# S4 and a dense mixture of experts on one core: the waits of S4's kernel chain, rewritten

## The chip, the core and the metric

The kernel runs on one core of a Trainium2 chip. Its engines work side by side, each through its own instructions in order: TensorE (matrix products; PE in the profile, its weight loads PEld), VectorE (DVE), ScalarE (ACT), GpSimd (POOL) and SyncE (SP), which here issues most of the DMAs. Products land in PSUM banks and are read out by ScalarE or VectorE. The metric is the device time of the whole kernel in microseconds; less is better.

## The reference

The input is one sequence of 2048 tokens of 512 channels. It is normalized, and the output is the sum of the input, an S4 branch and a mixture of experts:

```python
x = A_u
xn = _layernorm(x, axis=-1)
return x + _A_ref(xn, ...) + _B_ref(xn, B_w_gate, B_w1, B_w2)

# _A_ref: S4, a convolution over time for each channel, and a skip
P = exp(dt * A * arange(L));  K = einsum("dn,dnl,dn->dl", Cc, P, dB).real
y = irfft(rfft(up) * rfft(Kp))[:L] + u * Dskip
# _B_ref: K = E = 8, so each token goes through each of the 8 experts
gates = softmax(xf @ w_gate)
out = sum over e of gates[:, e] * (silu(xf @ w1[e]) @ w2[e])     # F = 1792
```

The change touches only the S4 branch: how the convolution kernel K (with the skip added at its first tap) is scaled and handed on.

## The kernel before

**Two works in one program.** The mixture of experts is nearly all of TensorE's work: 8 experts by 4 blocks of 512 tokens, each block in four parts of hidden columns (DQS: 2, 2, 2 and 1 pairs), each part in four slots. A slot issues one or two sets of first products (`product`, hb), a few second products (`pop`, y), and the activations between. 512 slots cover the whole, and `clock["slot"]` counts them; `now()` returns the count. All operands are split into a high and a low f16 part, so a product is three matmuls, and each tensor needs a high part (ScalarE) and a low part (VectorE).

**S4 beside it.** S4 goes in 32 chunks of 16 channels (NCH = 32). Its instructions are put into the queues while the mixture's slots are written out: at the end of each slot from the 46th on, `bg_run` first polls the small generators in `polled` once each, in order (`s4_pe` first), and then draws VectorE work from the generator `bg` until a quota is used up: SHARE = 0.905 of the TensorE time that the planner counts for the slot, less the VectorE time that it counts for the mixture. So the whole order is fixed when the program is written out, and no engine can overtake it. What is left of S4 before the last token block of the last expert is put out by `bg_until("s4")` with no mixture work between (line 1335 ff.; called in the main loop at the end).

**One chunk c.** VectorE makes tables (`s4_tables`, from a basis made for every two chunks). TensorE forms the kernel product kgen from them (`s4_kernel`, L803) in the small bank, the one PSUM buffer with the tag s4, which all of S4's products share (ps_s, bufs=1). ScalarE copies it to ksb (`s4_kernel_out`, L810), VectorE adds the skip (`s4_skip`, L816), and `s4_kernel_turn` squares ksb for its sum per partition (L822) and turns the tile over DRAM (kd, then four loads kt: L826, L828). `pow2_total` sums the rows over the partitions with a product with ones (L180) and gives, after its read (L175), the scale (`s4_kscale`, L186 to L191). Then come the high and low part of the turned kernel (`s4_khigh` L841, `s4_klow` L846), its transform (`s4_kf`, L884), the convolution on VectorE (`s4_conv`, L899 to L937), the split of its result z (`s4_zhigh`, `s4_zlow`), the back product (`s4_back`, L958) and the output (`s4_out`). The input's transform is `s4_uf` (L870).

**Waits in slots.** S4's order is made by generators that yield until a key was set enough slots ago. `until(key, more=m)` goes on once now() > slot of the key + m; without m that is two slots later. `hold(stamp)` goes on once the slot is past stamp. A bare `yield None` is one slot. `bank_wait` waits until the small bank's last product was read out: `bank_free` puts the pending read into ScalarE's queue and says yes one slot later. Since one bank serves all, `s4_pe` puts its products in a fixed cycle: kf(c), back(c-1), kernel(c+2), uf(c+1). The wait in front of kernel(c+2), line 1045, is

```python
yield from until(("kl", c + 1), more=-1)
```

with "kl" set by s4_klow, the low part of the chunk before. `s4_ksplit(c)` runs the steps from the copy to the low part, line 1064 ff., and is one of the polled generators; `s4_dve(c)` waits for "kn" (the kernel product of the chunk before, since the tables have one buffer), makes tables(c+2), waits for "kf" and runs the convolution of c.

Of the kernel before, what the change touches and what calls it, by code (L numbers as in the profile page):

```python
# [9 lines left out]
F32 = mybir.dt.float32  # L10
F16 = mybir.dt.float16
BF16 = mybir.dt.bfloat16
I32 = mybir.dt.int32
AF = mybir.ActivationFunctionType
ALU = mybir.AluOpType
AX = mybir.AxisListType
PSUM = bass.MemoryType.PSUM

P = 128
# [14 lines left out]
def s4_moe_kernel(  # L34
# [15 lines left out]
    nc = tc.nc  # L50
    V, S, T = nc.vector, nc.scalar, nc.tensor
# [10 lines left out]
    NCH = us.shape[0]  # L62
    DC = 16
    NI = NT
# [3 lines left out]
    cp = ctx.enter_context(tc.tile_pool(name="cp", bufs=1))  # L68
    sb = ctx.enter_context(tc.tile_pool(name="sb", bufs=2))
# [31 lines left out]
    clock = {"slot": 0, "pe": 0.0, "pe0": 0.0, "dve": 0.0, "dve0": 0.0, "left": 0.0,  # L101
             "act": 0.0, "act0": 0.0, "pe1": 0.0, "actleft": 0.0, "two": False}
# [33 lines left out]
    wgt = cp.tile([P, KT, E], F32, name="wgt")  # L136
    dskq = cp.tile([P, NCH, 4], F32, name="dskq")
    V.memset(dskq, 0.0)
    sgnt = cp.tile([P, 2], F32, name="sgnt")
    mult_t = cp.tile([P, 2, NK], F32, name="mult_t")  # L140
    dt_all = cp.tile([P, D], F32, name="dt_all")
# [498 lines left out]
    s4 = {}  # L640
# [11 lines left out]

    def s4_twiddle():

        f = s4["angle"] = sb.tile([P, P + 1], F32, tag="b0", name="angle", bufs=1)
        V.tensor_copy(f, s4["odd"])

        def sines():
            tw = s4["tw"] = sb.tile([P, 2, P + 1], F32, tag="b1", name="twid", bufs=1)
            S.activation(tw[:, 1], f, AF.Sin, scale=math.pi / (4 * P))  # L660
            S.activation(tw[:, 0], f, AF.Sin, scale=-math.pi / (4 * P), bias=halfpi)
        act_later.append((clock["slot"] + 1, sines))
# [132 lines left out]
    def s4_kernel(c):  # L795
        tb = s4["tb", c]
        take_bank(lambda: s4_kernel_out(c))
        kg_ = ps_s.tile([P, 4, 64], F32, tag="s4", name=f"kgen{c}")
        for dg in range(4):
            for cc in range(2):  # L800
                for dsb in range(4):
                    d = dsb * 4 + dg
                    T.matmul(kg_[32 * dsb:32 * dsb + 32, dg, :], tb[:, cc, 0, d, :],  # L803
                             tb[:, cc, 1:3, d, :], start=(cc == 0), stop=(cc == 1))
        s4["kgen"] = kg_
        clock["pe"] += 1.2

    def s4_kernel_out(c):
        ksb = s4["ksb"] = sb.tile([P, 8, 4, NS], F32, tag="ksb", name=f"ksb{c}", bufs=1)
        S.copy(ksb, s4["kgen"].rearrange("p g (j m) -> p j g m", j=8))  # L810
        clock["act"] += at_(256)
        s4["kc", c] = now()

    def s4_skip(c):

        V.tensor_tensor(s4["ksb"][:, 0, :, 0], s4["ksb"][:, 0, :, 0], dskq[:, c, :], op=ALU.add)  # L816

    def s4_kernel_turn(c):
        ksb = s4["ksb"]
        row = s4["krow", c] = sb.tile([P, 1], F32, tag="krow", name=f"krow{c}", bufs=2)  # L820
        junk = sb.tile([P, 2, DC * NI], F16, tag="kh", name=f"ksq{c}", bufs=1)
        S.activation(junk[:, 0].bitcast(BF16), ksb.rearrange("p j g m -> p (j g m)"), AF.Square, accum_out=row)  # L822
        clock["act"] += at_(256)
        kt = sb.tile([P, 4, 4 * NI], F32, tag="kt", name=f"kt{c}", bufs=1)
        kd = kds[c % 2]
        nc.sync.dma_start(kd, ksb.rearrange("p (j r) g m -> p j (r g m)", r=2))  # L826
        for jh in range(4):
            nc.sync.dma_start(kt[32 * jh:32 * jh + 32],  # L828
                              kd[:, jh, :].rearrange("(s x) c -> x s c", s=4))
        s4["kt", c] = kt.rearrange("p s x -> p (s x)")  # L830

    def s4_kscale(c):


        ks = s4["ks", c] = sb.tile([P, 2], F32, tag="ksc", name=f"ksc{c}", bufs=4)
        pow2_scale(ks[:, 0:1], s4["kst", c], f"k{c}")
        pow2_inverse(ks[:, 1:2], ks[:, 0:1], ZSH - DSH)
# [39 lines left out]
    def s4_kf(c):  # L877
        take_bank()
        kf = ps_s.tile([P, 2, 2, DC * NS], F32, tag="s4", name=f"kf{c}")
        kh = s4["kh", c].rearrange("p y (s r x) -> p y r s x", s=4, r=2)  # L880
        for a in range(2):
            for r in range(2):
                for n, (x, y) in enumerate(((0, 0), (1, 0), (0, 1))):
                    T.matmul(kf[:, a, r], dfth[:, x, 4 * r + 1 - a, :], kh[:, y, r],  # L884
                             start=(n == 0), stop=(n == 2))
        clock["pe"] += 0.68
        k4 = sb.tile([P, 4, 2, DC, NS], F32, tag="k4", name=f"k4{c}", bufs=1)
        S.copy(k4[:, 2:4].rearrange("p a r d i -> p (a r d i)"), kf.rearrange("p a r d -> p (a r d)"))
        bank["at"] = now()
        s4["k4", c] = k4  # L890
# [59 lines left out]
    def s4_back(c):  # L950
        zh = s4["zh", c]
        take_bank(lambda: s4_out(c))
        yp = ps_s.tile([P, 2, DC, NS], F32, tag="s4", name=f"yp{c}")
        for r in range(2):
            n = 0
            for a in range(2):
                for x, y in ((0, 0), (1, 0), (0, 1)):
                    T.matmul(yp[:, r].rearrange("p d i -> p (d i)"), dfth[:, x, 4 * r + 2 + a, :], zh[:, y, a, r],  # L958
                             start=(n == 0), stop=(n == 5))
                    n += 1  # L960
        s4["yp", c] = yp
        clock["pe"] += 0.68
# [8 lines left out]
    def at_(n):  # L971

        return n / 1050 + 0.17
# [5 lines left out]
    def hold(stamp):  # L979

        while clock["slot"] <= stamp:
            yield None

    def now():
        return clock["slot"]
# [28 lines left out]
    def bank_wait():  # L1014
        while not bank_free():
            yield None

    def until(*keys, more=1):

        for key in keys:  # L1020
            while key not in s4 or now() <= s4[key] + more:
                yield None

    def s4_pe():


        for c in range(-2, NCH + 1):
            if 0 <= c < NCH:
                if c:
                    yield from until(("z at", c - 1))  # L1030
                yield from until(("kl", c))
                yield from bank_wait()
                s4_kf(c)
                s4["kf", c] = now()
                yield None
            if c > 0:
                yield from until(("zl", c - 1))
                yield from bank_wait()
                s4_back(c - 1)
                s4["back", c - 1] = now()  # L1040
                yield None
            if c + 2 < NCH:
                yield from until(("tab", c + 2))
                if c > -2:
                    yield from until(("kl", c + 1), more=-1)
                yield from bank_wait()
                s4_kernel(c + 2)
                s4["kn", c + 2] = now()
                polled.append(s4_ksplit(c + 2))
                yield None  # L1050
                yield from bank_wait()
                yield from until(("kc", c + 2))
            if 0 <= c + 1 < NCH:
                if c >= 0:
                    yield from until(("v3", c))
                yield from until(("ul", c + 1))
                yield from bank_wait()
                s4_uf(c + 1)
                s4["uf", c + 1] = now()
                yield None  # L1060
        yield from bank_wait()
        done.add("s4")

    def s4_ksplit(c):

        yield from until(("kc", c), more=0)
        s4_skip(c)
        yield 0.2
        yield from hold(now() + 1)
        if c:  # L1070
            yield from until(("kf", c - 1), more=0)
        s4_kernel_turn(c)
        yield None
        yield from hold(now())
        yield from bank_wait()
        s4["kst", c] = pow2_total(s4["krow", c], 1, f"k{c}", lambda: s4.update({("read", c): now()}))
        s4["total", c] = now()
        yield None
        while ("read", c) not in s4:
            bank_free()  # L1080
            if ("read", c) not in s4:
                yield None
        yield from until(("read", c), more=0)
        s4_kscale(c)
        yield 0.6
        yield None
        if c:
            yield from until(("kf", c - 1), more=0)
        s4_khigh(c)
        yield None  # L1090
        yield None
        s4_klow(c)
        s4["kl", c] = now()
        yield tt_(256)
# [77 lines left out]
    for pr in range(3, NPR):  # L1172
        for h in range(2):
            n = 2 * (pr - 3) + h
            tag, bufs = ("sE", 1) if n == 0 else ("sCB", 3) if n < 4 else ("stg", 4)
# [593 lines left out]
```

## Time and profile before

| | |
|---|---|
| time, median of 3 runs | 2445.02 us (2444.57 to 2445.96) |
| profiled execution | 2446.37 us; span 2444.6 us, first to last instruction |
| PE busy | 2331.7 us, 95% of the span |
| VectorE busy | 1751.4 us, 72% |
| ScalarE busy | 1464.6 us, 60% |
| GpSimd busy | 339.2 us, 14% |
| granted TensorE clock, mean | 0.974 of full speed |

A row of a timeline is: start in us, duration in us, engine, line, operation, output<-inputs, shape, count; in brackets the idle time before it and what ended it. A row by stretch has, for each engine, its busy time and its instructions in brackets. A row of the groups has a count, the busy time, the mean in ns of one, and then the idle time of the engine before them. The time strip cuts the span into 40 slices of 61 us and gives each engine's busy tenths. A row of waits is: who waited, for whom, us in total, times, longest.

### The profile page before, as it was taken

How to read it: one execution, taken by the hardware profiler on the slowest of the kernel's cores; microseconds unless marked ns; L12 is line 12 of the kernel's file. 1: busy time of each engine (PE TensorE's matmuls, PEld its weight loads, DVE VectorE, ACT ScalarE, POOL GpSimd, SP SyncE). 2: the span in 40 equal slices, each digit the busy share in tenths (PEclk: the TensorE clock that was granted, in tenths of full speed). 3: DMA queues.
4: the chain of work that ended last, by engine and by line, in shares of the span. 5: the costliest groups of instructions: out<-in, count | busy, mean ns of one | idle time of the engine just before them, and what ended most of it. 6: DMA issues, size and time to landing. Idle time of an engine off the chain costs nothing. (4 is left out here: it accounts for less than half of the span.)

```text
span 2444.6 us, 46072 instructions
## 1 busy us (share of the span) xinstructions
PE 2331.7 (95%) x18289; PEld 1559.0 (64%) x18289; DVE 1751.4 (72%) x3492; ACT 1464.6 (60%) x2587; POOL 339.2 (14%) x396
## 2 busy tenths in 40 slices
PE   8999999999999999999999999999999999995259
PEld 4666666666666666666666666666666666664135
DVE  8855875768946797767966697658876588757951
ACT  7676765657666576556666566665665576543123
POOL 0001011120122111011111111111111111110012
PEclk9999999999999999999999999999999999997579
DMA  7686555655667466545666455654655554442127
GB/s 263 193 252 173 143 138 123 149 96 144 147 139 155 80 149 152 127 100 116 142 139 141 84 142 138 137 118 93 147 131 131 120 132 94 76 87 53 22 33 177
DMA packets 325433, 316.33 MB, mean 129 GB/s; under 512 B 183584, under 2 KB 219936, under 8 KB 324768
## 3 DMA queue, kind: packets, MB, share of 16 engines
q1 hardware_dynamic: 268768, 219.24, 30.7%
q0 software_dynamic: 55872, 93.61, 24.3%
q8 instruction: 143, 2.34, 0.4%
q14 instruction: 74, 0.61, 0.1%
q10 hardware_dynamic: 576, 0.52, 0.1%
HBM read 201.88 MB, written 66.06 MB: 110 GB/s over the span
## 5 line engine op out<-in xcount | busy, mean ns | idle before, releaser
L1406 PE MATMUL hb<-xop,w1s 128*128 128x256 f16 x9114 | 1074.1, 273 | 0.4 <-ACT scC L1625 0.3
L1406 PEld LDWEIGHTS <-w1s 128*128 128x128 f16 x9114 | 882.9, 98 | 176.6 <-issue 1.9
L1389 PE MATMUL y<-w2s,ahl 128*128 128x512 f16 x1792 | 679.6, 379 | 0.0
L1390 PE MATMUL y<-w2s,ahl 128*128 128x512 f16 x1792 | 679.4, 379 | 0.0
L1391 PE MATMUL y<-w2s,ahl 128*128 128x512 f16 x1792 | 679.4, 379 | 0.0
L1391 PEld LDWEIGHTS <-ahl 128*128 128x128 f16 x1792 | 175.4, 98 | 211.7 <-issue 0.6
L1596 POOL DMA_DIRECT2D scC<-sE x124 | 116.4, 939 | 1286.3 <-ACT sE L1625 1122.7
L1435 DVE SCALAR_TENSOR_TENSOR ahl<-fa,sc,ahl 128x512 f16<-128x512 f32 (+1 forms) x262 | 179.0, 684 | 154.8 <-ACT ahl L1426 154.2
L1390 PEld LDWEIGHTS <-ahl 128*128 128x128 f16 x1792 | 175.4, 98 | 161.5 <-issue 0.3
L1389 PEld LDWEIGHTS <-ahl 128*128 128x128 f16 x1792 | 175.4, 98 | 161.4 <-issue 0.3
L1422 ACT ACTIVATE fa<-hb,sc 128x512 f32<-128x512 f32 (+1 forms) x252 | 160.5, 637 | 194.7 <-PE hb L1406 194.2
L1435 DVE SCALAR_TENSOR_TENSOR ahl<-scB,sc,ahl 128x512 f16<-128x512 f32 x124 | 84.6, 682 | 196.4 <-ACT ahl L1426 173.7
L1640 ACT COPY hb<-hb 128x512 f32<-128x512 f32 x124 | 64.1, 517 | 234.9 <-PE hb L1406 234.7
L1435 DVE SCALAR_TENSOR_TENSOR ahl<-scC,sc,ahl 128x512 f16<-128x512 f32 x124 | 84.5, 681 | 160.4 <-ACT ahl L1426 146.4
L1426 ACT ACTIVATE ahl<-fa,sc 128x512 f16<-128x512 f32 (+1 forms) x262 | 175.7, 671 | 8.5
L1630 ACT COPY hb<-hb 128x512 f32<-128x512 f32 x124 | 64.3, 519 | 179.5 <-PE hb L1406 179.2
L1596 POOL DMA_DIRECT2D scB<-sE x124 | 107.2, 865 | 415.1 <-ACT scB L1625 307.2
L785 DVE TENSOR_TENSOR ta<-tb,zr 128x64 f32<-128x64 f32 (+2 forms) x192 | 131.8, 687 | 6.0
L791 DVE TENSOR_TENSOR tb<-ta,tt 128x64 f32<-128x64 f32 (+2 forms) x192 | 132.0, 688 | 5.6
L925 DVE TENSOR_TENSOR s<-s,tm 128x672 f32<-128x672 f32 (+6 forms) x224 | 127.7, 570 | 7.8
L788 DVE TENSOR_TENSOR tt<-tb,zi 128x64 f32<-128x64 f32 (+2 forms) x192 | 130.5, 680 | 0.0
L1367 POOL DMA_DIRECT2D oacc<-ye x108 | 95.8, 1331 | 247.4 <-ACT ye L1364 245.7
(267 smaller groups left out, 2547.0 us busy)
## 6 DMA issues: line engine op xcount, KB each, us to landing
xop<-xd SPq DMA_DIRECT2D x210, 256.0 KB, 3.6
pp<-in_w_dram SPq DMA_DIRECT2D x98, 512.0 KB, 4.3
raw<-in_w_dram SPq DMA_DIRECT2D x56, 512.0 KB, 5.1
oacc<-ye POOLq DMA_DIRECT2D x108, 256.0 KB, 6.2
scC<-sE POOLq DMA_DIRECT2D x93, 256.0 KB, 4.3
scB<-sE POOLq DMA_DIRECT2D x93, 256.0 KB, 4.0
raw<-in_w_dram SPq DMA_DIRECT2D x52, 256.0 KB, 4.1
raw<-in_w_dram SPq DMA_DIRECT2D x104, 128.0 KB, 4.0
```

The lines of the kernel that those rows point to most:

```text
L785: V.tensor_tensor(ta, tin, zrv, op=ALU.mult)
L788: V.tensor_tensor(tt, tin[:, ::-1], ziv, op=ALU.mult)
L791: V.tensor_tensor(tout, ta, tt, op=ALU.add)
L925: V.tensor_tensor(s3[:, :, m:], s3[:, :, m:], tm, op=ALU.add)
L1389: T.matmul(y, lhs[0], w2s[pr][:, 0, fh, :], start=(c == 0), stop=False)
L1390: T.matmul(y, lhs[0], w2s[pr][:, 1, fh, :], start=False, stop=False)
L1391: T.matmul(y, lhs[1], w2s[pr][:, 0, fh, :], start=False, stop=(c == NF - 1))
L1406: T.matmul(dst[:, q, :], w1s[pr][:, a, wo, k * P:(k + 1) * P], xop[:, xo, b, k, :], start=(first_mm and q == 0 and n == 0), stop=(n == 5), ...
L1422: S.activation(fa, src[:, :n], AF.Silu, scale=w1_unscale(e, d if whole else prs[0]))
L1426: S.activation(ahl[:, 0, :n], fa, AF.Copy, scale=scales[e][:, 3:4])
L1435: V.scalar_tensor_tensor(ahl[:, 1, :n], fa, sc[:, 3:4], ahl[:, 0, :n], op0=ALU.mult, op1=ALU.subtract)
L1596: nc.gpsimd.dma_start(dst, src, accum_op=ALU.add)
```

## The change

The square that gives the kernel's sum per partition is taken from the small bank, at the copy, ahead of the skip; its elementwise output goes to ksb and is overwritten by the copy. The sum of the skip's squares, made once for all chunks (dsk2), is added to the row when the skip is added. So the sum is that of the squares of kernel and skip, and no longer that of the squares of their sum; it only sets a power of two for scaling. In ksplit a hold is shortened, a bare yield and a second hold go, and the turn waits for the low part of the chunk before (kl) and no longer for its transform (kf). In s4_pe the next kernel product waits for the turn ("ke", a new key) and the read of the total ("read") of the chunk before, and no longer for its low part ("kl").

```diff
+    dsk2 = cp.tile([P, NCH], F32, name="dsk2")
...
     def s4_twiddle():
+        q = sb.tile([P, NCH, 4], F32, tag="b2", name="dskx", bufs=1)
+        V.tensor_tensor(q, dskq, dskq, op=ALU.mult)
+        V.tensor_reduce(dsk2, q, axis=AX.X, op=ALU.add)
...
     def s4_kernel_out(c):
         ksb = s4["ksb"] = sb.tile([P, 8, 4, NS], F32, tag="ksb", name=f"ksb{c}", bufs=1)
+        row = s4["krow", c] = sb.tile([P, 1], F32, tag="krow", name=f"krow{c}", bufs=2)
+        S.activation(ksb.rearrange("p j g m -> p (j g m)"), s4["kgen"].rearrange("p g x -> p (g x)"), AF.Square, accum_out=row)
         S.copy(ksb, s4["kgen"].rearrange("p g (j m) -> p j g m", j=8))
-        clock["act"] += at_(256)
+        clock["act"] += 2 * at_(256)
         s4["kc", c] = now()
...
     def s4_skip(c):
+        row = s4["krow", c]
         V.tensor_tensor(s4["ksb"][:, 0, :, 0], s4["ksb"][:, 0, :, 0], dskq[:, c, :], op=ALU.add)
+        V.tensor_tensor(row, row, dsk2[:, c:c + 1], op=ALU.add)
...
     def s4_kernel_turn(c):
         ksb = s4["ksb"]
-        row = s4["krow", c] = sb.tile([P, 1], F32, tag="krow", name=f"krow{c}", bufs=2)
-        junk = sb.tile([P, 2, DC * NI], F16, tag="kh", name=f"ksq{c}", bufs=1)
-        S.activation(junk[:, 0].bitcast(BF16), ksb.rearrange("p j g m -> p (j g m)"), AF.Square, accum_out=row)
-        clock["act"] += at_(256)
         kt = sb.tile([P, 4, 4 * NI], F32, tag="kt", name=f"kt{c}", bufs=1)
...
         s4["kt", c] = kt.rearrange("p s x -> p (s x)")
+        s4["ke", c] = now()
...
                 if c > -2:
-                    yield from until(("kl", c + 1), more=-1)
+                    yield from until(("ke", c + 1), ("read", c + 1), more=0)
                 yield from bank_wait()
                 s4_kernel(c + 2)
...
         yield from until(("kc", c), more=0)
         s4_skip(c)
-        yield 0.2
-        yield from hold(now() + 1)
+        yield 0.3
+        yield from hold(now())
         if c:
-            yield from until(("kf", c - 1), more=0)
+            yield from until(("kl", c - 1), more=0)
         s4_kernel_turn(c)
-        yield None
-        yield from hold(now())
         yield from bank_wait()
         s4["kst", c] = pow2_total(s4["krow", c], 1, f"k{c}", lambda: s4.update({("read", c): now()}))
```

More of the change, by code (lines that the diff above doesn't have):

```diff
@@ L827, in s4_kernel_turn @@
         for jh in range(4):
-            nc.sync.dma_start(kt[32 * jh:32 * jh + 32],
-                              kd[:, jh, :].rearrange("(s x) c -> x s c", s=4))
+            nc.sync.dma_start(kt[32 * jh:32 * jh + 32], kd[:, jh, :].rearrange("(s x) c -> x s c", s=4))
         s4["kt", c] = kt.rearrange("p s x -> p (s x)")
+        s4["ke", c] = now()
     def s4_kscale(c):
```

## The prediction

> **What bounds the kernel now.** I read the time strip of the page first, then the busy time by stretch, then TensorE's order at the seam, then who waits for whom.
>
> ```profile
> PE   8999999999999999999999999999999999995259
> DVE  8855875768946797767966697658876588757951
> ```
>
> TensorE is full up to slice 36 and then has three poor slices of 61 us each. The same stretches in numbers (columns: length, then busy us of PE, weight loads, VectorE, ScalarE, GpSimd, then granted clock, DMA share, GB/s):
>
> ```profile
> 400.00:2200.00 1800.00, 1799.57 (x14240) 1210.30 (x14239) 1318.31 (x2563) 1121.96 (x2004) 277.55 (x318) 1.00 0.56 125
> 2229.90:2354.30 124.40, 25.24 (x353) 21.99 (x352) 111.09 (x235) 17.52 (x41) 0.21 (x1) 0.51 0.11 19
> 2248.00:2284.00 36.00, 6.41 (x101) 5.62 (x101) 33.80 (x70) 3.68 (x11) 0.00 (x0) 0.50 0.10 15
> 2284.00:2314.00 30.00, 6.41 (x101) 5.62 (x101) 28.14 (x57) 4.31 (x11) 0.00 (x0) 0.50 0.12 18
> ```
>
> From 400 to 2200 us TensorE never rests and VectorE has a quarter of its time free. From 2229.9 to 2354.3 it is the reverse: this is bg_until("s4"), which empties the rest of S4 before the last token block, with no MoE work to lie beside it. VectorE sets the pace there (33.80 of 36 us, then 28.14 of 30). TensorE's rows at the two edges, and the kernel products between:
>
> ```profile
> 313.11 1.10 PE L803 MATMUL kgen<-tb 128*32 128x64 f32 x64
> ...
> 2211.72 1.10 PE L803 MATMUL kgen<-tb 128*32 128x64 f32 x64
> ...
> 2229.07 0.83 PE L958 MATMUL yp<-zh,dfth 128*128 128x128 f16 x12
> ...
> 2314.45 1.93 PE L803 MATMUL kgen<-tb 128*32 128x64 f32 x64 [14.19 <-ACT st_k L175]
> ...
> 2352.94 1.59 PE L958 MATMUL yp<-zh,dfth 128*128 128x128 f16 x12 [12.19 <-ACT ysb L966]
> 2354.32 2.77 PE L1406 MATMUL hb<-xop,w1s 128*128 128x256 f16 x12
> ```
>
> So of 32 chunks 29 had their kernel product before the seam (the first at 313, the 29th at 2211.72), three came after it, and the seam costs 2354.3 - 2229.7 = 124.6 us. How fast S4 runs beside the MoE decides how much is left there: 28 periods took (2211.72 - 313.11) / 28 = 67.8 us each.
>
> What sets that period? One chunk in mid-kernel, in order of time: its kernel product, uf, the square, the total, the low part of its transform, and then the next kernel product and the first step of VectorE's next tables:
>
> ```profile
> 1186.90 1.10 PE L803 MATMUL kgen<-tb 128*32 128x64 f32 x64
> ...
> 1202.27 0.83 PE L870 MATMUL uf<-uh,dfth 128*128 128x128 f16 x12
> 1202.94 0.27 PE L1406 MATMUL hb<-xop,w1s 128*128 128x256 f16 x1
> ...
> 1213.20 0.40 ACT L822 ACTIVATE ksq<-ksb 128x256 bf16<-128x256 f32 x1
> ...
> 1221.86 0.17 PE L180 MATMUL tot_k<-krow,ones 128*128 128x1 bf16 x1
> 1221.89 0.81 PE L1406 MATMUL hb<-xop,w1s 128*128 128x256 f16 x6
> ...
> 1245.06 0.48 DVE L846 SCALAR_TENSOR_TENSOR kh<-kt,ksc,kh 128x256 f16<-128x256 f32 x1
> ...
> 1253.22 1.10 PE L803 MATMUL kgen<-tb 128*32 128x64 f32 x64
> ...
> 1255.45 0.07 DVE L765 MEMSET tb<- 128x16 f32 x1
> ```
>
> One period is 1253.22 - 1186.90 = 66.3 us. VectorE begins the next tables at 1255.45, behind the product at 1253.22 (the tables have one buffer, which that product reads), and the product by the old rule waits for the low part at 1245.06. VectorE is out of S4 work meanwhile: it was busy 39.08 of 41 us before this hole and 3.99 of 19 us in it, with TensorE full in both:
>
> ```profile
> 1195.00:1236.00 41.00, 41.00 (x294) 26.89 (x292) 39.08 (x72) 27.04 (x49) 3.44 (x4) 1.00 0.59 146
> 1236.00:1255.00 19.00, 19.00 (x193) 13.34 (x192) 3.99 (x7) 12.59 (x23) 1.81 (x3) 1.00 0.45 111
> ```
>
> So S4 is held by a chain of one-slot waits, not by work.
>
> **The old chain in slots.** The waits are written in slots, so I count them in the code. (A step whose key must be one slot old comes at +1, by until's default at +2.) With the kernel product in slot K: its copy K+1, skip K+2, then hold(now() + 1) and the turn with the square K+5; uf K+3, kf K+4, back product K+5; a bare yield and a hold, K+7, where ksplit itself releases the bank that the back product left; total K+8, read K+9, scale K+10, high part K+12, low part K+14. s4_pe is polled ahead of ksplit, so it sees the low part at K+15: the next kernel product. Fifteen slots in 66.3 us make 4.42 us a slot; the mean of 67.8 us has a slot added here and there, where another total wants the bank.
>
> **The change, part by part.**
> 1. Square from the small bank at K+1, ahead of the copy, and gone from the turn. ScalarE does as many instructions as before. L822 took 0.40 us from SBUF; read from PSUM I bound it by nothing saved and 0.4 us more, and take the same. It holds the bank less than 1 us longer inside a slot of 4.42 us. What it removes: ScalarE's square no longer stands behind VectorE's skip.
> 2. The row add and dsk2: one small VectorE instruction per chunk. Its nearest rows are below (L816, 159 ns), so 32 x 0.16 = 5 us of VectorE over the whole kernel, plus two once; bounds 2 and 10 us. Hidden under TensorE in the MoE stretch.
> 3. hold(now()), no bare yield and no second hold: the turn is at K+4 at the earliest and the total can follow in the same slot. At K+4 kf has just taken the bank, at K+5 the back product; released by ksplit at K+5, so the total is at K+6, its read K+7: two slots won.
> 4. The turn now waits for the low part of the chunk before (it reuses kt). The recurrence low part to low part is turn +1, read +2, scale +3, high +5, low +7: 7 slots, so it allows 31 us.
> 5. The next kernel product stands behind turn and read: K+8 instead of K+15. That is the large edit.
> The turn moves its five DMAs on SP with it. They are as many as before; kd still has its skip two slots ahead, and kt must be there four slots (17.7 us) after the turn instead of seven. SP waits on the kd write 112.4 us over 32 turns, 3.5 us each, and kt lands 1.8 us after issue, so the cover holds; were it gone, ScalarE would stand at the high part. The rows for 2 and for this, from the groups by line, SyncE's waits, the view of tile kt and TensorE's waits:
>
> ```profile
> L816 DVE TENSOR_TENSOR ksb<-ksb,dskq 128x4 f32<-128x4 f32 x32 | 5.1, 159 | 2.0 <-ACT ksb L810 1.9
> SPq L828 <- DMA kd<-ksb: 112.4, 32, 8.5
> DMA to landing us min/median/max: 1.6/1.8/4.1
> PE hb L1406 <- ACT scC L1625: 0.3, 1, 0.3
> ```
>
> **What is late next.** With the product allowed at K+8 the tables of the chunk after are ready too late for that: VectorE's work becomes the limit. Uncontended it needed 33.80 us for a chunk with a basis and 28.14 us without, 31 us on average. In the MoE stretch 1800 / 67.8 = 26.5 chunks took 26.5 x 31 = 822 us of 1318, so the MoE takes 496 / 1800 = 0.276 of VectorE. At the 39.08 / 41 = 0.953 that it reached in the dense part, a chunk needs 31 / (0.953 - 0.276) = 45.8 us, or 10.4 slots. TensorE's order must fit into that. Counted from the slot Z in which a convolution ends: z's high part Z+1, its low part Z+3, back product Z+5 (two behind its key), bank released and kernel product Z+7, its copy Z+8, uf Z+10, total Z+11, and the next kf behind the next convolution's end by two, so Z+12 or Z+13. It fits, with up to a slot lost where total and kf meet at the bank: **10.5 to 12 slots, 47 to 53 us.**
>
> Does S4 then end before the seam? From the first kernel product to the seam are 2229.7 - 313.1 = 1917 us. After the last kernel product two convolutions without tables remain; by the waits above 3 + 8 + 8 + 7 = 26 slots, 115 us. At 50 us the need is 31 x 50 + 115 = 1665 us, 250 us in hand. The break-even period is (1917 - 115) / 31 = 58 us, 13.1 slots. So all of S4 hides, and the rest of the speed is worth nothing.
>
> **The sum**, on the profiled execution (2446.4 us, span 2444.6; the median of the runs, 2445.0, is 1.4 lower):
> - the seam goes: -124.6;
> - its TensorE work comes to lie between MoE products: 3 kernel products at 1.10, 4 uf, 4 kf and 5 back products (as large as a uf) at 1202.94 - 1202.27 = 0.67, 4 totals at 1221.89 - 1221.86 = 0.03: 3.3 + 8.7 + 0.1 = +12.1;
> - after the seam TensorE started at half clock (0.51 granted): 12 products took 2.77 us. By the rows at 1202.94 (1 in 0.27) and 1221.89 (6 in 0.81) a further one is 0.108 us, so 12 take 1.46: -1.3.
>
> 2446.4 - 124.6 + 12.1 - 1.3 = 2332.6; less 1.4 for the median: **2331 us**.
>
> **The rivals.**
> - **S4 gets faster, but not enough** (7 in 100): a wait that I missed keeps 14 slots, 62 us. Before, 31 x 67.8 + 115 - 1917 = 300 us too much became a seam of 124.6. At 62 us there are 120 too much, so 50 us of seam, worth 45 net: 2376. For it: stretches in which the bank is shared with the weights' totals. Against: it needs over 13.1 slots, and I count at most 12.
> - **VectorE runs late and TensorE feels it** (small form, 5 in 100): dense for some 1500 us instead of two thirds of each period. In the dense 41 us above TensorE had no gap, and the only wait of the MoE products on ScalarE is the 0.3 us shown. A stall of 1% there, which I set as its size, is 15 us: 2346.
> - **The same, beyond the gain** (slower, 4 in 100): at the low parts of the activations (L1435), which the y products need. It decides where stalls pass the 114 us won, in 1500 us, 7.6%. That needs a VectorE demand of 1.08 of its time; at a period of 46 us mine is (31 + 0.276 x 46) / 46 = 0.95. At 10% it would be 2331 + 150 = 2481.
> - **GpSimd's adds starve** (2 in 100). They are the accumulating DMAs scC and scB, each issue 0.86 us and at most 1.92 us, by the view of tile scC:
>
> ```profile
> L1596 POOL DMA_DIRECT2D scC<-sE x124: 859/859/1917, 97.2 to 2422.0; - x124
> DMA to landing us min/median/max: 2.7/4.2/11.8
> ```
>
> If a dense VectorE doubled each landing, ScalarE would take scC later, and a stall of, say, 0.2 us in each of some 170 adds (two per block of 17.6 us) is 34 us: 2365. The Trainium skill, "SBUF — State Buffer", section "SBUF: two separate sides", speaks for this rival: VectorE in a 2-port mode locks GpSimd out, so that it can't write descriptors. By that rule the added load would show in the issue times. The trace agrees little: the median equals the minimum.
> - **It doesn't do what it says** (3 in 100): the planner's VectorE quota, not the chain, holds the period; 2445. Against: the 19 us with VectorE at 3.99.
>
> **How the numbers follow.** All of S4 hidden, without stalls: 79 in 100, and 2320 to 2340 as its own range (the floor is the sum without the 12.1). The small stalls bring it to 84, and the range reaches to 2352 for them; the others stay out. About 0.2%, 5 us, is what a measurement of this kernel can tell from no change. Faster: 79 + 7 + 5 + 2 = 93; same 3; slower 4.
>
> **What would show it.** Right: strip of PE at 9 through slice 38; kernel products 47 to 53 us apart; no idle stretch before the last block; VectorE at 9 until about 1950 us and then at 3 or 4. Right in 3 and 5: total six to eight slots ahead of where it was, product next to VectorE's convolution end. Wrong: products still 62 us or more apart (a wait missed), or TensorE's waits on ahl, hb copies or scC over 10 us in total (VectorE or ScalarE late).

## The result, and the profile after

| | before | changed |
|---|---|---|
| median | 2444.80 us of 4 runs | 2334.26 us of 4 runs (2332.68 to 2335.29) |
| ratio to before, 95% interval | | 0.9547 (0.953 to 0.9563) |
| span of the profiled execution | 2444.6 us | 2332.7 us |

The change saves 110.5 us; 2331 was forecast. First the page of the changed kernel, the lines of PE and VectorE: busy time and share, then the strip of 40 slices (58 us each now).

```profile
PE 2317.6 (99%) x18289; PEld 1547.9 (66%) x18289; DVE 1747.6 (75%) x3526; ACT 1467.5 (63%) x2587; POOL 340.4 (15%) x396
...
PE   8999999999999999999999999999999999999999
...
DVE  8864889889998999888999889999899741441111
```

TensorE's three poor slices are gone. VectorE does the same work (1747.6 us against 1751.4) but stands at 8 or 9 from slice 5 to slice 31 and is nearly idle at the end. In stretches (length; then PE, weight loads, VectorE, ScalarE, GpSimd busy; clock, DMA share, GB/s):

```profile
400.00:1750.00 1350.00, 1348.37 (x11270) 912.46 (x11268) 1216.17 (x2469) 870.23 (x1578) 207.77 (x237) 1.00 0.59 129
1950.00:2230.00 280.00, 280.00 (x1895) 185.08 (x1894) 79.41 (x113) 150.86 (x251) 42.75 (x49) 1.00 0.40 88
2244.50:2332.70 88.20, 84.07 (x535) 52.17 (x533) 14.79 (x26) 34.08 (x60) 24.92 (x29) 0.99 0.67 147
```

While S4 lasts VectorE is busy 1216 of 1350 us, 90%, where it was 73%; afterwards 28%. The last token block is the third row: it begins at 2244.5, straight behind the block before, instead of at 2354.3, and its first 12 products take 1.47 us instead of 2.77. The first and the last kernel product of S4, its last back product and the first products of the last block, from TensorE's timeline:

```profile
313.24 1.10 PE L807 MATMUL kgen<-tb 128*32 128x64 f32 x64
...
1823.27 1.10 PE L807 MATMUL kgen<-tb 128*32 128x64 f32 x64
...
1925.38 0.83 PE L962 MATMUL yp<-zh,dfth 128*128 128x128 f16 x12
...
2244.51 1.47 PE L1408 MATMUL hb<-xop,w1s 128*128 128x256 f16 x12
```

The mean period is (1823.27 - 313.24) / 31 = 48.7 us, and S4 is over at 1926 us, 318 us ahead of the last block. One period from the middle, all engines, in order of time:

```profile
816.38 1.10 PE L807 MATMUL kgen<-tb 128*32 128x64 f32 x64
...
820.72 0.39 ACT L815 ACTIVATE ksb<-kgen 128x256 f32<-128x256 f32 x1
...
824.03 0.42 DVE L941 TENSOR_TENSOR z<-zq 128x256 f32<-128x256 f32 x1
...
825.96 0.15 DVE L824 TENSOR_TENSOR krow<-krow,dsk 128x1 f32<-128x1 f32 x1
...
826.73 0.07 DVE L769 MEMSET tb<- 128x16 f32 x1
...
831.34 0.48 DVE L850 SCALAR_TENSOR_TENSOR kh<-kt,ksc,kh 128x256 f16<-128x256 f32 x1
...
840.24 0.17 PE L181 MATMUL tot_k<-krow,ones 128*128 128x1 bf16 x1
...
867.03 1.10 PE L807 MATMUL kgen<-tb 128*32 128x64 f32 x64
```

Read it against the old period: VectorE ends a convolution at 824.45 and begins the next tables at 826.73, since the product that frees the tables' buffer came at 816.38. The low part of the chunk before (831.34) now falls behind that product. The square (L815) stands ahead of the copy. TensorE's waits over the whole kernel:

```profile
PE tp L357 <- ACT xhl L347: 7.2, 1, 7.2
PE hb L1408 <- ACT scC L1627: 1.6, 6, 0.5
PE hb L1218 <- POOL ident masks.py:199: 1.4, 1, 1.4
```

Only the second of these is new in size: 1.6 us in six places where it was 0.3 in one.

### The profile page after: what moved, and what is told of

It reads as the page before. It is cut to its first block, busy times and chain, and to the rows that moved or that the text cites. A ratio compares the mean times of both kernels' runs of the same rounds, so it can differ in the third digit from the quotient of the medians.

```text
span 2332.7 us, 46118 instructions
## 1 busy us (share of the span) xinstructions
PE 2317.6 (99%) x18289; PEld 1547.9 (66%) x18289; DVE 1747.6 (75%) x3526; ACT 1467.5 (63%) x2587; POOL 340.4 (15%) x396
## 4 chain that ended last, share of the span: by engine, by line
PE 97%; ACT 2%; DVE 0%; issue 0%; DMA 0%; SPq 0%; DVEq 0%; ACTq 0%
PE hb L1408 42%; PE y L1393 16%; PE y L1392 16%; PE y L1391 16%; PE hb L1680 2%; PE kgen L807 1%; PE uf L874 1%; PE kf L888 1%; PE yp L962 1%; ACT ye L1366 1%; PE tp L282 0%; ACT ahl L1428 0%; DMA ut0c<-in_u_dram 0%; ACT scB L1424 0%; ACT fa L1424 0%
## 5 line engine op out<-in xcount | busy, mean ns | idle before, releaser
L1437 DVE SCALAR_TENSOR_TENSOR ahl<-fa,sc,ahl 128x512 f16<-128x512 f32 (+1 forms) x262 | 178.9, 683 | 138.4 <-ACT ahl L1428 137.8
L1437 DVE SCALAR_TENSOR_TENSOR ahl<-scB,sc,ahl 128x512 f16<-128x512 f32 x124 | 84.5, 682 | 165.9 <-ACT ahl L1428 164.4
L1437 DVE SCALAR_TENSOR_TENSOR ahl<-scC,sc,ahl 128x512 f16<-128x512 f32 x124 | 84.4, 681 | 127.3 <-ACT ahl L1428 122.9
```

The source lines that it names most:

```text
L1437: V.scalar_tensor_tensor(ahl[:, 1, :n], fa, sc[:, 3:4], ahl[:, 0, :n], op0=ALU.mult, op1=ALU.subtract)
```

## The experiments

The theory to be tried, called the pace theory below: the time depends on one number, the mean period p of the kernel products beside the mixture. What 31 p + 115 us exceeds 1917 us by is left over at the last block, 0.41 us of seam for each us, nine tenths of it lost; below 58 us nothing is won any more. Its first rival: each edit pays its share of the slots that it saves.

### The square alone

The kernel before, with the change's edits of s4_twiddle, s4_kernel_out and s4_skip (dsk2 among them), and in s4_kernel_turn only this:

```diff
-        row = s4["krow", c] = sb.tile([P, 1], F32, tag="krow", name=f"krow{c}", bufs=2)
-        junk = sb.tile([P, 2, DC * NI], F16, tag="kh", name=f"ksq{c}", bufs=1)
-        S.activation(junk[:, 0].bitcast(BF16), ksb.rearrange("p j g m -> p (j g m)"), AF.Square, accum_out=row)
-        clock["act"] += at_(256)
```

> The kernel before with only the square moved: taken from the small bank at the copy, the skip's squares added to the row; all waits as before. Pace theory: no wait in slots is shortened, so the period stays 67.8 us and the time 2445 us (2441 to 2449). Rival, the square behind the skip held the chain: some us less per period, 2430 us or less.

Measured: 2446.31 us, ratio 1.0006 (0.9997 to 1.0016). Moving the square is worth nothing by itself. By the code the new turn needs it all the same: the old square's junk tile takes kh's one buffer, which the transform of the chunk before still reads, so a turn ahead of that transform must not write it.

### The one wait alone

The kernel before, with two edits:

```diff
         s4["kt", c] = kt.rearrange("p s x -> p (s x)")
+        s4["ke", c] = now()
...
-                    yield from until(("kl", c + 1), more=-1)
+                    yield from until(("ke", c + 1), ("read", c + 1), more=0)
```

> The kernel before with only the one wait changed: the next kernel product stands behind the turn and the read of the total of the chunk before. Square at the turn, both holds, and the turn behind the transform of the chunk before stay as they were. Pace theory: the total comes later (turn behind kf, then three slots), yet the read is done before VectorE's tables call for the product, so the period is 48 to 53 us and the time 2334 us (2330 to 2340). Rival, the shorter chain in ksplit is needed as well: a period of over 58 us and a seam, 2350 us or more.

Measured: 2332.65 us, ratio 0.9544 (0.9528 to 0.956), the whole gain. The period is (2021.43 - 312.82) / 31 = 55.1 us by these rows of TensorE's timeline, two to seven us longer than I expected but under 58, and S4 ends at 2144.5 us:

```profile
312.82 1.10 PE L803 MATMUL kgen<-tb 128*32 128x64 f32 x64
...
2021.43 1.10 PE L803 MATMUL kgen<-tb 128*32 128x64 f32 x64
...
2143.70 0.83 PE L959 MATMUL yp<-zh,dfth 128*128 128x128 f16 x12
```

So the shorter chain in ksplit is not needed for the gain. VectorE is busy 83% from 400 to 1650 us here (1040 of 1250), less than its quota of 0.905 allows, so a wait still holds this period; which one is open.

### All but that wait: 13, 14 and 15 slots

The changed kernel, with the old key put back; more is -1 here, 0 in the second run, 1 and 2 in the last two:

```diff
-                    yield from until(("ke", c + 1), ("read", c + 1), more=0)
+                    yield from until(("kl", c + 1), more=-1)
```

> The changed kernel with one line put back: the next kernel product waits for the low part of the chunk before again; square, holds and turn stay as changed. Pace theory (the time depends only on the period p of the kernel products: what 31 p + 115 us exceeds 1917 us by becomes a seam of 0.41 us per us, worth nine tenths of that): product 13 slots after the last one instead of 15, 57.5 us and 1.5 us for slots lost at the bank, 59 us; 27 us too much, a seam of 11 us, 2344 us (2332 to 2352). Rival, each edit pays its share of the slots: 2 slots of 7 give two sevenths of the 110 us won, 2413 us.

Measured: 2343.87 us, ratio 0.9587 (0.9572 to 0.9601): without the wait, the other edits bring 101 of the 110 us. The period is (2164.82 - 312.46) / 31 = 59.8 us. Just over the break-even, a rest of S4 is left; the first and the last kernel product, the last back product and the first product of the last block:

```profile
312.46 1.10 PE L807 MATMUL kgen<-tb 128*32 128x64 f32 x64
...
2164.82 1.10 PE L807 MATMUL kgen<-tb 128*32 128x64 f32 x64
...
2250.21 1.59 PE L962 MATMUL yp<-zh,dfth 128*128 128x128 f16 x12 [6.57 <-ACT ysb L970]
2251.60 2.76 PE L1408 MATMUL hb<-xop,w1s 128*128 128x256 f16 x12
```

> As the run with the product behind the low part, and one slot later still: 14 slots. Pace theory: 62 us and 1.5 us lost at the bank, 63.4 us; 31 x 63.4 + 115 - 1917 = 163 us too much, a seam of 68 us, worth 61: 2395 us (2375 to 2410). Rival, each edit pays its share: one slot of 7, 2429 us.

Measured: 2343.39 us, ratio 0.9586 (0.9571 to 0.96). This run was a mistake of mine: s4_pe is polled ahead of ksplit, so it can't see the key in the slot in which it is set, and more=0 gives the same order as more=-1 (TensorE's order is the same in both traces). It is a repetition of the run above and agrees within 0.5 us.

> The changed kernel with the next product behind the low part and one slot later than in the first of these runs, now truly one (the form with more=0 gives the same order as more=-1, since s4_pe is polled ahead of ksplit). Pace theory: the first run had a period of 59.8 us at 13 slots, so 14 slots give 64.2 us; 31 x 64.2 + 115 - 1917 = 188 us too much, a seam of 78 us, worth 70, less the 10 us by which the same sum overrated the first run: 2395 us (2380 to 2410). Rival, each edit pays its share: 2429 us.

Measured: 2417.16 us, ratio 0.9885 (0.987 to 0.9899), above the expected range. The 30th product is the last one beside the mixture; the 31st already waits alone:

```profile
2224.86 1.10 PE L807 MATMUL kgen<-tb 128*32 128x64 f32 x64
2255.76 1.93 PE L807 MATMUL kgen<-tb 128*32 128x64 f32 x64 [16.36 <-ACT st_k L176]
```

With the first at 314.19 the period is (2224.86 - 314.19) / 29 = 65.9 us, not 64.2: a slot more costs 6.1 us of period here, not 4.4. With the measured period the sum gives 2332 + 0.9 x 0.41 x (31 x 65.9 + 115 - 1917) = 2421. The miss was mostly in the period. (For the run with 13 slots the sum gives 2351 at the measured period, 7 us too much, not the 10 that I took off.)

> The same, one slot later again: 15 slots with the square, the holds and the turn as changed. Pace theory: the old period of 65 to 69 us is back with all other edits in place, and so is the old time, 2445 us (2430 to 2455). Rival: square, holds and turn are worth something by themselves, under 2425 us.

Measured: 2463.33 us, ratio 1.0074 (1.0059 to 1.0089). With this one wait stretched to 15 slots the changed kernel is slower than the one before, all other edits in place; the period is 69.5 us (28th product at 2190.68, first at 313.30), and the sum gives 2462; that is 8 us above the range that I had set. So at the same number of slots the square, the holds and the turn win nothing. Their worth is the two slots that they take out of the chain, and these alone bring nine tenths of the gain, as the run with 13 slots shows: that run is the kernel before with all edits but the one wait.

### VectorE's quota

The changed kernel with 0.70, and in further runs 0.80, 1.00 and 1.10:

```diff
-    SHARE = 0.905
+    SHARE = 0.70
```

> The changed kernel with VectorE's quota cut to 0.70. Pace theory: some 2.0 us of VectorE for S4 in a slot, 31.7 planned for a chunk, so 15.6 slots or 69 us a chunk in spite of the short chain; 337 us too much, a seam of 138 us: 2450 us (2435 to 2470). Rival: the chain of waits is what counts, the quota is not: below 2400 us.

Measured: 2474.30 us, ratio 1.0121 (1.0106 to 1.0136), 4 us above the range. The short chain is fully there, yet the kernel is slower than before: S4 lacks VectorE time and a rest is left, as the strip of VectorE shows: 6 or 7 through the middle, and 9 and 8 in slices 37 and 38, at the seam.

```profile
DVE  8854776777777776777776777777676777769851
```

> The changed kernel with VectorE's quota at 0.80. Pace theory: 2.48 us of VectorE for S4 in a slot, 12.8 slots, 56 to 58 us, just under the break-even of 58 to 59 us: hidden, 2331 to 2340 us. If a denser VectorE costs TensorE something at 0.905 already, this is 1 to 2 us faster than the changed kernel; if not, the same within 1 us.

Measured: 2331.36 us (2331.18 to 2331.71), ratio 0.9533 (0.9519 to 0.9546): the fastest of all. The period is (2069.61 - 336.26) / 31 = 55.9 us.

> The changed kernel once more, on the same chip and in the same rounds as its neighbours: 2334 us (2332 to 2336). It is the measure for a difference of one or two us.

Measured: 2334.53 us (2333.63 to 2335.27), ratio 0.9545 (0.9531 to 0.9558). So the changed kernel is 3.2 us slower at 0.905 than at 0.80, and the runs of the two don't overlap.

> The kernel before with only the wait of the next kernel product changed, once more. It was 1.6 us below the changed kernel, at a period of 55 us instead of 49. If less crowding is worth that, it comes out 1 to 2 us below the changed kernel again; if that was chance, within 1 us of it.

Measured: 2333.17 us (2331.81 to 2334.74), ratio 0.954 (0.9526 to 0.9553). That is 1.4 us below the changed kernel, as expected, but their runs overlap; I leave it open. It is also 1.8 us above the kernel at 0.80 (1.3 in the run before), with VectorE busy 83% in both.

> The changed kernel with VectorE's quota for S4 raised from 0.905 to 1.10 of TensorE's planned time. Pace theory: the quota would allow a chunk in 39 us, VectorE needs 43 us beside the mixture, the ring of products about 44 us; VectorE is at 98% while S4 lasts, S4 ends earlier, which is worth nothing, and TensorE feels little: 2334 to 2345 us. Rival, VectorE late: its queue falls behind and TensorE waits for the low parts of the activations, above 2350 us.

Measured: 2402.07 us, ratio 0.9826 (0.981 to 0.9842). My expectation failed and the rival came out: 68 us more than the changed kernel, though S4 ended far ahead (its last kernel product at 1695.39). What ScalarE waits for, the rows that name S4's and the weights' VectorE results:

```profile
ACT zi L747 <- DVE bf L744: 42.9, 8, 9.0
...
ACT zh L947 <- DVE z L941: 31.9, 13, 6.7
...
ACT w1s L491 <- DVE tw L504: 21.3, 7, 5.2
```

And TensorE's longest waits in that kernel:

```profile
PE kf L888 <- ACT st_k L176: 11.8, 2, 5.9
PE hb L1408 <- ACT scC L1627: 10.7, 10, 4.2
```

VectorE falls behind; ScalarE, which works in order, stands at a basis step (zi), at a convolution's split (zh) or at a weight split (w1s) that needs its result; behind these stand its reads of the small bank and the copies that free hb, and TensorE waits for ScalarE. By the list for 400 to 1650 us TensorE waits 23.5 us there ahead of S4's own products (kf, kgen, tot_k) for a read of the small bank, and 17.3 us ahead of hb. In the changed kernel there is no row of ScalarE waiting for z or bf, and 5.5 us for tw.

> The changed kernel with VectorE's quota at 1.00. At 1.10 the cost was 68 us, through ScalarE standing at S4's steps that need VectorE (zh at z, zi at bf), so that hb is freed late. VectorE was busy 90% of the stretch at 0.905 and 94% at 1.10. Theory, ScalarE at VectorE's results: the cost begins once VectorE's queue runs a slot late; 2338 to 2375 us with waits of ScalarE on z and bf in between those of the two neighbours. Rival, the cost at 1.10 was something else, a meeting of a few places: 2334 us, no such waits.

Measured: 2359.13 us, ratio 0.9648 (0.9634 to 0.9661), in between, with the same two rows between their neighbours':

```profile
ACT zh L947 <- DVE z L941: 13.9, 7, 3.5
ACT zi L747 <- DVE bf L744: 11.1, 4, 4.3
```

TensorE waits 13 us ahead of hb there, and 5.9 us for VectorE itself, ahead of a back product and a total.

The stretch from 400 to 1650 us, the same columns as above, for 0.80, 0.905, 1.00 and 1.10:

```profile
400.00:1650.00 1250.00, 1249.81 (x10196) 843.44 (x10194) 1035.34 (x2065) 798.15 (x1439) 194.48 (x222) 1.00 0.58 131
```

```profile
400.00:1650.00 1250.00, 1248.56 (x10430) 844.92 (x10428) 1127.74 (x2283) 808.65 (x1468) 195.45 (x223) 1.00 0.60 131
```

```profile
400.00:1650.00 1250.00, 1230.53 (x10414) 831.57 (x10413) 1176.35 (x2399) 795.57 (x1452) 188.98 (x216) 1.00 0.59 129
```

```profile
400.00:1650.00 1250.00, 1206.98 (x10190) 815.46 (x10191) 1173.12 (x2384) 783.01 (x1426) 183.92 (x212) 0.98 0.57 125
```

VectorE is busy 83%, 90%, 94% and 94%, and TensorE idle 0.2, 1.4, 19.5 and 43 us. From 1.00 to 1.10 VectorE does no more work in this stretch and the period stays at 45.5 us; the larger quota only makes TensorE wait longer, and TensorE's clock begins to drop (0.98).

All in one table, p from the kernel products beside the mixture, the sum as given above:

| kernel | p, us | time, us | sum, us |
|---|---|---|---|
| quota 0.80 | 55.9 | 2331.4 | 2332 |
| one wait alone | 55.1 | 2332.7 | 2332 |
| changed | 48.7 | 2334.3 | 2332 |
| quota 1.00 | 45.5 | 2359.1 | 2332 |
| quota 1.10 | 45.5 | 2402.1 | 2332 |
| behind the low part, 13 slots | 59.8 | 2343.9 | 2351 |
| 14 slots | 65.9 | 2417.2 | 2421 |
| quota 0.70 | 67.4 | 2474.3 | 2438 |
| before | 67.8 | 2444.8 | 2443 |
| square alone | 67.8 | 2446.3 | 2443 |
| 15 slots | 69.5 | 2463.3 | 2462 |

With the quota at 0.905 the sum is right within 8 us (the row of the kernel before agrees by construction: 0.41 and 0.9 come from it). It fails at 0.70, 1.00 and 1.10, so the period is not the one number. At 1.00 and 1.10 it leaves out what VectorE's lateness costs. At 0.70 it is 36 us short: the first kernel product comes at 356.34 us, 43 us later than in the kernel before, the 29th only as the seam begins (2226.90), and the seam is 155.9 us long. The late start is worth 0.9 x 0.41 x 43 = 16 us by the sum's price; the other 20 us are open.

## Why the prediction was right

**What bounds the kernel: right.** The seam was the whole prize. From the 13-slot kernel to the 14-slot one, 6.1 us of period cost 73 us, 12.0 for each; the forecast's price was 31 x 0.41 x 0.9 = 11.4. By that measured slope the 14-slot kernel's 2417 reaches 2332 at 65.9 - 85 / 12.0 = 58.8 us: the break-even was put at 58.

**The old chain and its hole: right.** The wait for the low part kept VectorE idle; with it gone tables follow the convolution within 2.3 us. The one wait is enough: alone it brings the whole gain. But it is not needed for most of it. I called it the large edit, with seven slots, and gave two to the shorter holds; those two, at 13 slots against a break-even of 13.1 by my own count, bring 101 us without it. The seven slots did not come out either: the wait alone shortens the period by 12.7 us, 2.9 slots. That speed beyond 58 us is worth nothing is what the runs show.

**The small costs: right.** The square from the small bank took 0.39 us (0.40 was taken), the row add 0.15 (0.16). The total came 840.24 - 816.38 = 23.9 us behind its product, 5.4 slots, as counted (K+6). The last part of the forecast, which spoke of a total six to eight slots ahead, contradicted that count and was wrong.

**What is late next: right in size, in part by luck.** The period was 48.7 us for 47 to 53, and S4 was over at 1926 us for about 1950. I let VectorE fill to the 0.953 of its dense part and added slots for TensorE's order. It is the quota that holds the new period: 55.9, 48.7 and 45.5 us at 0.80, 0.905 and 1.00, with VectorE busy 83%, 90% and 94%. With 0.901 in place of 0.953 the forecast's own formula gives 31 / (0.901 - 0.276) = 49.6 us; with 0.953 it gave 45.8, and 45.5 is what the larger quotas reach, below the range. After the last kernel product came 103 us (1823.27 to 1926.2), where I took 115.

**The sum: 3 us short.** Its terms for TensorE are borne out: its busy time was to fall by 25.24 - 12.1 + 1.3 = 14.4 us, and fell from 2331.7 to 2317.6, by 14.1. (The seam by the rows shown is 2354.3 - 2229.9 = 124.4 us; I took 0.2 more.) With the quota at 0.80 the time is 2331.4. The other 3.2 us are, by the two profiles, 1.7 us in which TensorE is idle (1.2 of them between 400 and 1650 us) and 1.4 us in which it is busy longer with the same instructions. That a denser VectorE costs them is not shown: the one wait alone, with VectorE as busy as at 0.80, lies in between.

**The rivals.** Not fast enough: it did not happen, but the 13- and 14-slot kernels are that case, at its price. VectorE late: if the 3 us are its small form, it cost 3 where I set 15. Its large form does not come to pass at 0.905, but I had its place and its margin wrong. I put it at the low parts of the activations (L1437 now), which y needs, and let it decide at a VectorE demand of 1.08. The quotas of 1.00 and 1.10 show it at ScalarE, which stands in order at S4's and the weights' steps, so that the small bank and hb come free late (argued from the order of its queue and the two lists of waits); it costs 25 us more than the changed kernel at 94% of VectorE's time, and 68 us when still more is pushed in. My second statement of it, that 98% would do no harm, was wrong too. GpSimd's adds did not starve, by the view of tile scC in the changed kernel:

```profile
L1598 POOL DMA_DIRECT2D scC<-sE x124: 862/862/1770, 97.3 to 2310.0; - x124
...
DMA to landing us min/median/max: 2.7/4.3/11.2
```

The issue is 0.86 us, as before, and the landing 4.3 us where it was 4.2, with VectorE at 90%. The lock that the Trainium skill describes ("SBUF — State Buffer", "SBUF: two separate sides") does not show in these adds. It is tied to VectorE's 2-port modes; whether VectorE's S4 work, most of it operations with two inputs, ran in one, no run here shows, so the rule itself was not put to the test. That the quota and not the chain held the old period fell: at the same quota the period went from 67.8 to 48.7 us.

## What to carry to other kernels

Where side work is spread over a busy engine's time, work out the pace that just fits and compare it with what each chunk really waits for: here a chain of one-slot waits, where two slots less brought nine tenths of the gain and one long wait less all of it. Edits that shorten the same chain don't add up once the pace fits: test each alone and each left out. Beyond that, more speed is worth nothing, and pushing in more at quotas of 1.00 and 1.10 cost 25 and 68 us: choose the slowest pace that still ends in time (0.80 instead of 0.905 here). When a helper engine runs late, look also at what stands behind its results in the in-order queue of the next engine, not only at the results that the bound engine reads itself.

## What I had not expected

In this kernel VectorE can't be filled to its last few per cent for nothing, and its busy share alone does not tell the price: it is 94% at quotas of 1.00 and 1.10 alike, and the times are 25 and 68 us above the changed kernel's. Below that the share explains nothing that these runs show: between 400 and 1650 us TensorE idled 1.4 us with VectorE at 90%, but 1.2 us at 79% (13 slots), and 0.2, 0.6 and 2.2 us in three profiles at 83% (quota 0.80, and the one wait alone twice).

And a slot of wait has no fixed price: from 13 to 14 slots the period grew by 6.1 us and from 14 to 15 by 3.6, where a slot of the kernel before is 4.4 us. Why the two steps differ is open.
